# Batch 0's attention scores: key spans read in place from the whole keys, block maxima in a second product

## The chip, the cores and the metric

One core of one Trainium2 chip runs the kernel. A core has five engines with queues of their own: TensorE (PE in the profile, its weight loads PEld), VectorE (DVE), ScalarE (ACT), GpSimd (POOL) and SyncE (SP), which here only issues transfers. On-chip data lies in SBUF, 128 partitions wide; products land in PSUM, a small accumulator memory. The metric is the device time of one launch in microseconds (us), the median of several runs. The profile is that of one execution.

## The reference

Attention with a local window and a summary of every block, then a gated feed-forward layer with a short convolution:

```python
# q, k, v: (4 batches, 8 heads, 768 positions, 64), fp32
k_sum = k.reshape(B, H, 24, 32, D).max(axis=3)        # one key per block of 32
v_sum = v.reshape(B, H, 24, 32, D).mean(axis=3)
scores_l = scale * q @ k.T, kept where |pos_q - pos_k| < 16
scores_s = scale * q @ k_sum.T + log(32)
a = softmax(concat([scores_l, scores_s]))
x = (a @ concat([v, v_sum])) as (batch, position, 512)
h = relu(x @ w_in)                                    # 512 -> 1024
conv = 3-tap convolution of h along the positions, per channel
out = (h * sigmoid(conv)) @ w_out                     # 1024 -> 512
```

## The kernel before

**Chunks and pairs.** The work is cut into 8 chunks of 384 positions, two per batch (`c`, with `b, hf = divmod(c, 2)`). A chunk's attention goes over 4 pairs of heads (`p`), two heads on the two halves of the 128 partitions. A chunk of a pair has 6 query blocks of 64. A query block needs 96 keys around it (its span, `WK`) and the 24 block maxima (`NB`): 120 columns (`NK`).

**Scores.** Before the change every pair of every chunk has a tile `kw` of 6 x 120 columns: per query block its 96-key span, copied so that the spans overlap in memory, then the 24 maxima. In chunk 0 the spans are copied on chip from the whole keys of the pair (`k`, 784 columns, which lie in `spare`, borrowed space of the later tiles `xh` and `xl`) by DVE (pair 0) and POOL (pairs 1 to 3), at L213. From chunk 1 on SP loads them from memory with overlapping reads (L168). DVE reduces the whole keys to the maxima `ks` (L210) once per batch and pair; POOL copies these into all six blocks of `kw` (L217). `qk` then makes 12 products of 64 queries by 120 columns in fp32 (L260) into two PSUM tiles `pq`, one per head, of which two exist in all (tag `s`, `bufs=2`): the next pair's scores wait until DVE has read this pair's.

**After the scores.** DVE adds the mask and takes the maximum (L278), ACT does the exponentials (L288) and a small step for the sums (L296), DVE the reciprocal (L297), DVE (chunk 0) or POOL (later) the multiplication (L300). PE transposes the result (`pt`, L308), ACT or DVE copies it out (`aT`, L315, L313), and PE multiplies with the values (`xp`, L329). The output is split into two parts, `xh` and `xl`, for a three-product emulation of fp32 in the feed-forward layer: first layer `f1` (L404), the gate on ACT, DVE and POOL (L422 to L456), second layer `f2` (L473).

**Other work at the start.** The weights come as 64-bit words and are decoded and split on ACT, DVE and POOL (`decode`, L97 to L104, and `weights`, L127, L128): `w_in` in chunk 0's time, `w_out` in that of chunk 1. `warm` puts matmuls of zeros (`pw`, L78) between the others in chunk 0: 10 at the start, and some after each score, transpose and product.

**Order.** SP issues all loads of chunk 0 in the order of the string `LOADS` ("k0 q0 k1 q1 v0 k2 q2 a0 ..."). An attention step of half a pair has a slot `j`; a slot loads keys two pairs ahead, and makes the scores of its own pair. For chunks 0 and 1 a scheduler orders the instructions of every engine by its own estimates; from chunk 2 on PE's order is written out by hand (`manual_schedule`), the other engines' is still the scheduler's. A tile with `bufs=n` has n buffers that are handed round: the next user waits until the last reader is done.

```python
    spare = []
    for tag in ("xh", "xl"):
        t = sp.tile([P, 2, KL], F32, tag=tag, name=f"k_{tag}", bufs=2)
        spare += [t[:, 0, :], t[:, 1, :]]
```

Of the kernel before, what the change touches and what calls it, by code (L numbers as in the profile page):

```python
# [7 lines left out]
F32 = mybir.dt.float32  # L8
# [8 lines left out]
P = 128  # L17
WIN = 16
BLK = 32
NB = S // BLK  # L20
QB = 64
NQ = S // QB
WK = QB + 2 * WIN
NK = WK + NB
SP = S + 2 * WIN
NP = H // 2
CH = S // 2
CB = CH // QB
# [3 lines left out]
KL = S + WIN  # L32
# [18 lines left out]
def attention_ffn(ctx, tc, qT, kT, vT, v4, w_in, cwT, w_out, mask8, ident_in, out):  # L51
    nc = tc.nc
    cp = ctx.enter_context(tc.tile_pool(name="cp", bufs=1))
    sp = ctx.enter_context(tc.tile_pool(name="sp", bufs=2))
# [13 lines left out]

    idle = cp.tile([P, 512], mybir.dt.bfloat16, name="idle")
    nc.vector.memset(idle, 0.0)
    pw = ps.tile([P, 512], F32, tag="f2", name="pw", bufs=1)

    def warm(where, after=None):
        def go():
            for i in range(WARM.get(where, 0)):
                nc.tensor.matmul(pw, idle[:, :P], idle, start=True, stop=True)  # L78

        if after is None:  # L80
            go()
        else:
            with tc.issue_after(after):
                go()
# [48 lines left out]

    state = {}

    spare = []
    for tag in ("xh", "xl"):
        t = sp.tile([P, 2, KL], F32, tag=tag, name=f"k_{tag}", bufs=2)
        spare += [t[:, 0, :], t[:, 1, :]]

    def ins(x):
        return getattr(x, "ins", x)

    def window(ap, step, lead, run):

        return bass.AP(
            tensor=ap.tensor, offset=ap.offset, ap=[lead, [QB * step, CB], [1, run]]
        )

    def load_k(c, p):  # L150
        b, hf = divmod(c, 2)
        i = c * NP + p
        st = state[(c, p)] = {}
        if i == NP - 1:
            kw = sp.tile([P, 1024], F32, tag="stage", name=f"kw{i}", bufs=2)
            st["kw"] = kw[:, : CB * NK].rearrange("p (b k) -> p b k", b=CB)
        else:
            st["kw"] = sp.tile([P, CB, NK], F32, tag="kw", name=f"kw{i}", bufs=3)
        if hf == 0:
            if c == 0:  # L160
                k = spare[p]
            else:
                k = sp.tile([P, KL], F32, tag="kT", name=f"kT{i}", bufs=2)
            nc.sync.dma_start(k, kT[b, p, :, :KL])
            st["k"] = k
        if c:
            first = kT[b, p, :, hf * CH : hf * CH + WK]
            nc.sync.dma_start(st["kw"][:, :, :WK], window(first, 1, [SP, P], WK))  # L168

# [32 lines left out]
    def prep_pair(c, p):  # L202
        b, hf = divmod(c, 2)
        st = state[(c, p)]
        kw = st["kw"]
        if hf == 0:
            k = st["k"]
            ks = cp.tile([P, NB], F32, tag=f"ks{p}", name=f"ks{c * NP + p}")
            kv = k[:, WIN:KL].rearrange("p (n t) -> p n t", t=BLK)
            nc.vector.tensor_reduce(ks, kv, AX.X, ALU.max)  # L210
            state[("ks", b, p)] = ks
        if c == 0:
            (nc.gpsimd if p else nc.vector).tensor_copy(  # L213
                kw[:, :, :WK], window(k, 1, list(k.ap[0]), WK)
            )
        ks = state[("ks", b, p)]
        nc.gpsimd.tensor_copy(  # L217
            kw[:, :, WK:NK], ks.unsqueeze(1).to_broadcast([P, CB, NB])
        )

    def vmean_pair(c, p):

# [25 lines left out]
    def qk(c, p):  # L248


        st = state[(c, p)]
        n = c * NP + p
        pq = [
            ps.tile([P, 512], F32, tag="s", name=f"pq{n}_{h}", bufs=2) for h in range(2)
        ]
        for blk in range(CB):
            i, half = divmod(blk, 2)
            for h in range(2):
                r = slice(h * QB, (h + 1) * QB)
                last = nc.tensor.matmul(  # L260
                    pq[h][half * QB : (half + 1) * QB, i * NK : (i + 1) * NK],
                    st["q"][r, blk * QB : (blk + 1) * QB],
                    st["kw"][r, blk, :],
                    start=True,
                    stop=True,
                )
        if c == 0:
            warm(f"pq{p}", ins(last))
        softmax(n, c % 2, pq)

    def softmax(n, hf, pq):
        nm = sp.tile([P, 2, 3], F32, tag="nm", name=f"nm{n}", bufs=3)
        sm = sp.tile([P, 2, 3], F32, tag="sm", name=f"sm{n}", bufs=3)
        for h in range(2):
            a = sp.tile([P, 3, NK], F32, tag="a", name=f"a{n}_{h}", bufs=DEPTH + 2)
            state[("a", 2 * n + h)] = a
            for i in range(3):
                nc.vector.tensor_tensor_reduce(  # L278
                    a[:, i, :],
                    pq[h][:, i * NK : (i + 1) * NK],  # L280
                    mask[:, hf, i, :],
                    -0.125,
                    3.0e38,
                    ALU.add,
                    ALU.min,
                    nm[:, h, i : i + 1],
                )
                nc.scalar.activation(  # L288
                    a[:, i, :],
                    a[:, i, :],  # L290
                    AF.Exp,
                    bias=nm[:, h, i : i + 1],
                    scale=-1.0,
                    accum_out=sm[:, h, i : i + 1],
                )
        nc.scalar.activation(sm, sm, AF.Copy, bias=1e-9)  # L296
        nc.vector.reciprocal(sm, sm)  # L297
        for h in range(2):
            a = state[("a", 2 * n + h)]
            (nc.gpsimd if n >= NP else nc.vector).tensor_tensor(  # L300
                a, a, sm[:, h, :].unsqueeze(2).to_broadcast([P, 3, NK]), ALU.mult
            )
# [56 lines left out]
    def slot(j):  # L359

        if j % 2 == 0:
            n = j // 2 + 2
            if NP <= n < npair:
                load_k(*divmod(n, NP))
                load_vt(*divmod(n, NP))
            if NP <= j // 2 < npair:
                load_vm(*divmod(j // 2, NP))
            if j // 2 < npair:
                qk(*divmod(j // 2, NP))
        else:  # L370
            n = (j + 1) // 2
            if NP <= n + 1 < npair:
                load_q(*divmod(n + 1, NP))
            if n < npair:
                c, p = divmod(n, NP)
                if c:
                    vmean_pair(c, p)
                    load_v(c, p)
                prep_pair(c, p)
# [111 lines left out]
    for item in LOADS.split():  # L491
        what, n = item[0], int(item[1:] or 0)
        if what == "k":
            load_k(0, n)
        elif what == "q":
            load_q(0, n)
        elif what == "v":
            load_vt(0, n)
        elif what == "a":
            load_v(0, n)  # L500
        elif what == "w":
            raws[n] = load_in(n)
        else:
            nc.sync.dma_start(cw_words, cwT.bitcast(U32))

    prep_pair(0, 0)
    for j in range(2 * NP):
        slot(j)
# [177 lines left out]
```

## Time and profile before

| | |
|---|---|
| time, median of 3 runs | 404.95 us (404.81 to 405.63) |
| span of the profiled execution | 403.3 us |
| PE, busy share of the span | 96% |
| PE weight loads | 80% |
| DVE | 65% |
| ACT | 63% |
| POOL | 37% |
| transfers | 54.47 MB, mean 135 GB/s |

The span is the time from the first to the last instruction of one profiled execution; the time of a run is a little longer. A PE that is busy is not PE at its peak, since its matmuls overlap and their ends are modelled. In the rows of the profile an instruction stands as line, engine, operation, written tile <- read tiles, and what it waited for in brackets. A line number is that of the kernel before; L78 is the filler, L260 the scores, L404 and L473 the two layers.

### The profile page before, as it was taken

Reading aid. Unit: us, or ns where it says so; the run is one execution under the profiler, and the core shown is the slowest. Engines: PE = TensorE matmul, PEld = TensorE weight load, DVE = VectorE, ACT = ScalarE, POOL = GpSimd, SP = SyncE. Lnnn points to the kernel's source line nnn. Section 1 sums busy time; section 2 is a strip of 40 time slices with the busy share of each in tenths; the row PEclk is TensorE's granted clock in tenths of the full one; section 3 lists DMA queues with packets and bytes.
Section 4 is the critical chain, followed back from the end, with each engine's and each line's share of the span. In section 5 each row is a group of like instructions: output and inputs, shape, how many; then the busy total and the mean of one; then the engine's idle time right before and its main releaser. Section 6 shows DMA issues by size and latency. Waiting matters only on the chain.

```text
span 403.3 us, 8835 instructions
## 1 busy us (share of the span) xinstructions
PE 387.8 (96%) x3173; PEld 322.2 (80%) x3173; DVE 262.9 (65%) x777; ACT 255.8 (63%) x806; POOL 150.3 (37%) x179
## 2 busy tenths in 40 slices
PE   8989879999989999999999999999999999999996
PEld 3546558787768888888888888888888888999884
DVE  4889969998976665667765466466565655556200
ACT  3575699998876787766666778666666653343211
POOL 2316565377764234332333333332422242222200
PEclk9999799999899999999999999999999999999999
DMA  8999783666896784546233343334220000000011
GB/s 293 337 367 191 203 212 119 210 199 194 237 205 188 229 261 127 150 148 199 68 101 112 79 114 113 101 98 120 67 63 28 28 2 26 26 28 27 28 52 52
DMA packets 60715, 54.47 MB, mean 135 GB/s; under 512 B 24640, under 2 KB 51328, under 8 KB 60672
## 3 DMA queue, kind: packets, MB, share of 16 engines
q1 hardware_dynamic: 56928, 47.19, 41.2%
q10 hardware_dynamic: 3744, 6.73, 4.5%
q8 instruction: 25, 0.41, 0.5%
q14 instruction: 18, 0.15, 0.1%
HBM read 45.55 MB, written 6.29 MB: 129 GB/s over the span
## 4 chain that ended last, share of the span: by engine, by line
PE 85%; ACT 5%; DVE 3%; DMA 3%; POOL 2%; issue 1%; SPq 0%; DVEq 0%; POOLq 0%
PE f L473 33%; PE f L404 32%; PE pq L260 7%; PE xp L329 5%; PE pt L308 5%; PE pw L78 3%; ACT a L288 2%; DMA va<-v 2%; DMA k_xh<-kT 1%; POOL wout_lo L128 1%; DVE a L300 1%; POOL glo L456 0%; ACT wu_o L97 0%; ACT t L425 0%; PE pv L234 0%
## 5 line engine op out<-in xcount | busy, mean ns | idle before, releaser
L456 POOL TENSOR_TENSOR glo<-t,ghi 128x383 fp32r<-128x383 f32 (+1 forms) x64 | 66.3, 1037 | 138.3 <-ACT ghi L455 125.9
L404 PE MATMUL f<-xh,win_hi 128*128 128x384 f32 (+1 forms) x256 | 92.5, 361 | 0.9 <-ACT win_hi L127 0.9
L434 DVE SCALAR_TENSOR_TENSOR t<-f,cw,t 128x382 f32<-128x382 f32 (+3 forms) x128 | 78.8, 615 | 19.2 <-ACT t L425 16.6
L404 PE MATMUL f<-xl,win_hi 128*128 128x384 f32 (+1 forms) x256 | 87.9, 344 | 0.0
L404 PE MATMUL f<-xh,win_lo 128*128 128x384 f32 (+1 forms) x256 | 87.2, 341 | 0.0
L288 ACT ACTIVATE a<-a,nm 128x120 f32<-128x120 f32 x192 | 73.4, 384 | 12.3 <-DVE nm L278 12.1
L473 PE MATMUL f<-wout_lo,ghi 128*128 128x512 f32 x192 | 75.7, 394 | 1.6 <-POOL wout_lo L128 1.6
L473 PE MATMUL f<-wout_hi,ghi 128*128 128x512 f32 x192 | 76.4, 398 | 0.0
L473 PE MATMUL f<-wout_hi,glo 128*128 128x512 f32 x192 | 75.0, 391 | 0.0
L300 POOL TENSOR_TENSOR a<-a,sm 128x360 f32<-128x360 f32 x56 | 45.7, 837 | 45.6 <-ACT f L422 28.1
L451 ACT ACTIVATE t<-t 128x383 f32<-128x383 f32 (+1 forms) x64 | 33.6, 526 | 40.3 <-DVE t L434 39.6
L452 DVE SCALAR_TENSOR_TENSOR t<-t,f 128x383 f32<-128x383 f32 (+1 forms) x64 | 35.2, 552 | 29.6 <-ACT t L451 29.6
L404 PEld LDWEIGHTS f<-xh,win_hi 128*128 128x128 f32 x256 | 49.3, 192 | 5.1 <-ACT win_hi L127 1.2
L404 PEld LDWEIGHTS f<-xl,win_hi 128*128 128x128 f32 x256 | 49.2, 192 | 1.4 <-issue 0.3
L404 PEld LDWEIGHTS f<-xh,win_lo 128*128 128x128 f32 x256 | 48.9, 191 | 0.2
L278 DVE CUSTOM_DVE_ANT_0 a<-pq,mask 128x120 f32<-128x120 f32 x192 | 42.7, 275 | 1.5 <-PE pq L260 1.3
L473 PEld LDWEIGHTS f<-wout_lo,ghi 128*128 128x128 f32 x192 | 36.1, 188 | 7.9 <-POOL wout_lo L128 2.2
L473 PEld LDWEIGHTS f<-wout_hi,glo 128*128 128x128 f32 x192 | 36.1, 188 | 7.7
L473 PEld LDWEIGHTS f<-wout_hi,ghi 128*128 128x128 f32 x192 | 36.2, 188 | 7.0 <-issue 0.5
L315 ACT COPY aT<-pt 120x384 f32<-120x384 f32 x60 | 28.2, 470 | 20.7 <-PE pt L308 20.7
L422 ACT ACTIVATE f<-f 128x384 f32<-128x384 f32 (+1 forms) x64 | 30.4, 475 | 15.8 <-PE f L404 15.6
L308 PE MATMUL pt<-ident,a 128*120 128x128 f32 x192 | 33.7, 283 | 5.1 <-ACT aT L315 3.1
(59 smaller groups left out, 508.8 us busy)
## 6 DMA issues: line engine op xcount, KB each, us to landing
va<-v SPq DMA_DIRECT2D x32, 288.0 KB, 4.2
kw<-kT SPq DMA_DIRECT2D x28, 288.0 KB, 6.4
q<-qT SPq DMA_DIRECT2D x32, 192.0 KB, 4.5
out_dram<-ob ACTq DMA_DIRECT2D x24, 256.0 KB, 2.0
kT<-kT SPq DMA_DIRECT2D x12, 392.0 KB, 3.9
vt<-vT SPq DMA_DIRECT2D x12, 384.0 KB, 4.3
wo<-w_out SPq DMA_DIRECT2D x8, 512.0 KB, 5.3
raw_a<-w_in SPq DMA_DIRECT2D x6, 512.0 KB, 11.5
```

The source lines that it names most:

```text
L260: last = nc.tensor.matmul(pq[h][half * QB : (half + 1) * QB, i * NK : (i + 1) * NK], st["q"][r, blk * QB : (blk + 1) * QB], st["kw"][r, bl ...
L278: nc.vector.tensor_tensor_reduce(a[:, i, :], pq[h][:, i * NK : (i + 1) * NK], mask[:, hf, i, :], -0.125, 3.0e38, ALU.add, ALU.min, nm[:, h ...
L288: nc.scalar.activation(a[:, i, :], a[:, i, :], AF.Exp, bias=nm[:, h, i : i + 1], scale=-1.0, accum_out=sm[:, h, i : i + 1],)
L300: (nc.gpsimd if n >= NP else nc.vector).tensor_tensor(a, a, sm[:, h, :].unsqueeze(2).to_broadcast([P, 3, NK]), ALU.mult)
L308: last = nc.tensor.transpose(pt[:NK, i * P : (i + 1) * P], a[:, i, :], ident)
L404: last = nc.tensor.matmul(ph[:, :n], w[:, fc, cc, :], x[:, cc, :n], start=(cc == 0 and m == 0), stop=(cc == NCC - 1 and m == 2),)
L422: nc.scalar.activation(h[:, :n], h[:, :n], AF.Relu)
L434: nc.vector.scalar_tensor_tensor(t[:, i0:i1], h[:, hf + k - 1 + i0 : hf + k - 1 + i1], cw[:, fc, k : k + 1], t[:, i0:i1], ALU.mult, ALU.add,)
L451: nc.scalar.activation(t, t, AF.Tanh, scale=0.5)
L452: nc.vector.scalar_tensor_tensor(t, t, 1.0, h[:, hf : hf + ng], ALU.add, ALU.mult)
L456: nc.gpsimd.tensor_tensor(gated["lo"][:, fc, d0 : d0 + ng], t, hi.bitcast(F32), ALU.subtract)
L473: nc.tensor.matmul(po, gx[:, fc, ss], w[:, fc, :], start=(fc == 0 and m == 0), stop=(fc == NFC - 1 and m == 2),)
```

## The change

Batch 0 (chunks 0 and 1) has no `kw` any more. Its whole keys, all 800 columns with the margins, stay on chip for both chunks: pairs 0 and 1 in the two buffers of tag `kT`, pairs 2 and 3 in two of the three of tag `kw`. The scores are made in two products: 12 of 96 columns that read the span in place, then 12 of 24 columns that read `ks` itself, into the same places of `pq`. The span copies of chunk 0, the loads of chunk 1's spans and POOL's eight copies of the maxima for batch 0 go. From batch 1 on all is as before, except that `kT`'s and `kw`'s buffers first hold batch 0's keys. The tile of zeros for the filler shrinks from 512 to 128 columns, read four times over.

```diff
-    idle = cp.tile([P, 512], mybir.dt.bfloat16, name="idle")
+    idle = cp.tile([P, P], mybir.dt.bfloat16, name="idle")
...
-                nc.tensor.matmul(pw, idle[:, :P], idle, start=True, stop=True)
+                nc.tensor.matmul(
+                    pw.rearrange("p (r n) -> p r n", n=P),
+                    idle,
+                    idle.unsqueeze(1).to_broadcast([P, 4, P]),
...
-    spare = []
-    for tag in ("xh", "xl"):
-        t = sp.tile([P, 2, KL], F32, tag=tag, name=f"k_{tag}", bufs=2)
-        spare += [t[:, 0, :], t[:, 1, :]]
...  load_k
-        if i == NP - 1:
-            kw = sp.tile([P, 1024], F32, tag="stage", name=f"kw{i}", bufs=2)
+        if hf == 0:
+            tag, bufs = ("kw", 3) if b == 0 and p > 1 else ("kT", 2)
+            k = sp.tile([P, SP], F32, tag=tag, name=f"kT{i}", bufs=bufs)
+            n = SP if b == 0 else KL
+            nc.sync.dma_start(k[:, :n], kT[b, p, :, :n])
+            st["k"] = k
+        if b == 0:
+            st["k"] = state[(0, p)]["k"]
+        else:
+            kw = sp.tile([P, SP], F32, tag="kw", name=f"kw{i}", bufs=3)
             st["kw"] = kw[:, : CB * NK].rearrange("p (b k) -> p b k", b=CB)
-        else:
-            st["kw"] = sp.tile([P, CB, NK], F32, tag="kw", name=f"kw{i}", bufs=3)
-        if hf == 0:
-            if c == 0:
-                k = spare[p]
-            else:
-                k = sp.tile([P, KL], F32, tag="kT", name=f"kT{i}", bufs=2)
-            nc.sync.dma_start(k, kT[b, p, :, :KL])
-            st["k"] = k
-        if c:
             first = kT[b, p, :, hf * CH : hf * CH + WK]
             nc.sync.dma_start(st["kw"][:, :, :WK], window(first, 1, [SP, P], WK))
...  prep_pair
-        if c == 0:
-            (nc.gpsimd if p else nc.vector).tensor_copy(
-                kw[:, :, :WK], window(k, 1, list(k.ap[0]), WK)
-            )
-        ks = state[("ks", b, p)]
-        nc.gpsimd.tensor_copy(
-            kw[:, :, WK:NK], ks.unsqueeze(1).to_broadcast([P, CB, NB])
-        )
+        ks = state[("ks", b, p)]
+        if b:
+            nc.gpsimd.tensor_copy(
+                st["kw"][:, :, WK:NK], ks.unsqueeze(1).to_broadcast([P, CB, NB])
+            )
...  qk
+        if b == 0:
+            def near(r, blk):
+                at = hf * CH + blk * QB
+                return st["k"][r, at : at + WK]
+            ks = state[("ks", b, p)]
+            parts = [(0, WK, near), (WK, NK, lambda r, blk: ks[r, :])]
+        else:
+            parts = [(0, NK, lambda r, blk: st["kw"][r, blk, :])]
+        for first, end, keys in parts:
+            for blk in range(CB):
...
```

The scheduler makes another order of chunks 0 and 1 from this. Three places of it follow, with the tile's number behind each name (so `pq_0_132` is a score tile of the first head, `a_0` the softmax of the first head of a pair, `f_0_2` the first layer of chunk 0, block 2). The first is PE in chunk 0, the scores of the third pair (`q_2`) and the transposes of the first pair's two heads. Before:

```order
L78 MATMUL pw<-idle 128x512
L260 MATMUL pq_0_257<-kw_100,q_2_102 64x120
L308 MATMUL pt_235<-ident,a_0_153 120x128 x3
L78 LDWEIGHTS idle
...
L260 MATMUL pq_1_258<-kw_100,q_2_102 64x120
L260 MATMUL pq_0_257<-kw_100,q_2_102 64x120
...
L234 MATMUL pv_1_230<-ident,vs_1_228 24x128
L260 MATMUL pq_1_258<-kw_100,q_2_102 64x120
L308 MATMUL pt_247<-ident,a_1_160 120x128 x3
```

And the same place now:

```order
L78 MATMUL pw<-idle 128x512
L317 MATMUL pt_253<-ident,a_0_161 120x128 x3
L78 LDWEIGHTS idle
...
L267 MATMUL pq_0_271<-kT_98,q_2_100 64x96
L267 MATMUL pq_1_272<-kT_98,q_2_100 64x96
...
L229 MATMUL pv_1_248<-ident,vs_1_246 24x128
L267 MATMUL pq_1_272<-kT_98,q_2_100 64x96
L317 MATMUL pt_263<-ident,a_1_168 120x128 x3
```

The one product of the third pair that stood alone ahead of the first transposes has moved behind them, to the others; the 24-column products (`pq<-ks`) of this pair come after the second transposes.

The second place is SP's queue after the loads of `LOADS`: the span loads of chunk 1 before,

```order
L110 DMA raw_b<-w_in 128x1024 x2
L168 DMA kw_255<-kT 128x6x96
L185 DMA q_0_329<-qT 128x384
L168 DMA kw_343<-kT 128x6x96
L185 DMA q_1_415<-qT 128x384
L193 DMA va_417<-v 96x6x128
L168 DMA kw_521<-kT 128x6x96
L198 DMA va_417<-vm_0_175 24x6x128
```

and what follows there now:

```order
L116 DMA raw_b<-w_in 128x1024 x2
L184 DMA q_0_355<-qT 128x384
L184 DMA q_1_449<-qT 128x384
L192 DMA va_451<-v 96x6x128
L197 DMA va_451<-vm_0_183 24x6x128
L184 DMA q_2_601<-qT 128x384
```

The `kw` loads are gone, and queries and values have moved up by their places.

The third place is PE in chunk 1, around the scores of its third pair (`q_2`), with the first layer of chunk 0, blocks 1 and 2. Before:

```order
L404 MATMUL f_0_1_505<-xh_325,win_lo 128x384
L78 LDWEIGHTS idle
...
L404 MATMUL f_0_2_764<-xl_326,win_hi 128x384
L404 MATMUL f_0_2_764<-xh_325,win_lo 128x384
L308 MATMUL pt_600<-ident,a_0_540 120x128 x3
L404 MATMUL f_0_2_764<-xh_325,win_hi 128x384
...
L308 MATMUL pt_643<-ident,a_1_547 120x128 x3
L260 MATMUL pq_0_667<-kw_521,q_2_558 64x120
```

And now:

```order
L413 MATMUL f_0_1_538<-xh_351,win_lo 128x384
L78 LDWEIGHTS idle
...
L267 MATMUL pq_0_718<-kT_98,q_2_601 64x96
L317 MATMUL pt_652<-ident,a_0_583 120x128 x3
L267 MATMUL pq_0_718<-kT_98,q_2_601 64x96 x2
...
L267 MATMUL pq_0_718<-ks_261,q_2_601 64x24
...
L413 MATMUL f_0_2_826<-xh_351,win_hi 128x384
```

The third pair's scores have moved from behind most of block 2 of the first layer, and behind the transposes of both heads, to just behind block 1.

More of the change, by code (lines that the diff above doesn't have):

```diff
@@ L77, in go @@
             for i in range(WARM.get(where, 0)):
-                nc.tensor.matmul(pw, idle[:, :P], idle, start=True, stop=True)
+                nc.tensor.matmul(
+                    pw.rearrange("p (r n) -> p r n", n=P),
+                    idle,
+                    idle.unsqueeze(1).to_broadcast([P, 4, P]),
+                    start=True,
+                    stop=True,
+                )
         if after is None:
@@ L204, in prep_pair @@
         st = state[(c, p)]
-        kw = st["kw"]
         if hf == 0:
@@ L255, in qk @@
         ]
[L256 to L265, printed above, removed]
-                )
+        b, hf = divmod(c, 2)
+        if b == 0:
[8 more added lines that the diff above has]
+            for blk in range(CB):
+                i, half = divmod(blk, 2)
+                for h in range(2):
+                    r = slice(h * QB, (h + 1) * QB)
+                    last = nc.tensor.matmul(
+                        pq[h][
+                            half * QB : (half + 1) * QB, i * NK + first : i * NK + end
+                        ],
+                        st["q"][r, blk * QB : (blk + 1) * QB],
+                        keys(r, blk),
+                        start=True,
+                        stop=True,
+                    )
         if c == 0:
```

## The prediction

> **What bounds the kernel now.** I read the page first, then the stages, then the chain of waits over the first 30 us, then TensorE's (PE) timeline. The page:
>
> ```profile
> span 403.3 us, 8835 instructions
> PE 387.8 (96%) x3173; PEld 322.2 (80%) x3173; DVE 262.9 (65%) x777; ACT 255.8 (63%) x806; POOL 150.3 (37%) x179
> ```
>
> The sum below is made against this execution, 403.3 us of span; the median of the runs shown is 404.95 us, so 1.65 us lies around the span and is added at the end. The stages (us from:to, then length, busy time of PE, PE weight loads, DVE, ACT, POOL, the granted clock, DMA share, GB/s):
>
> ```profile
> 0.00:24.00 24.00, 22.17 (x179) 10.70 (x179) 16.55 (x58) 11.87 (x49) 6.66 (x15) 1.00 0.98 318
> 24.00:46.00 22.00, 17.31 (x176) 11.63 (x176) 20.98 (x61) 13.81 (x46) 10.47 (x9) 0.97 0.92 251
> 46.00:60.00 14.00, 11.06 (x109) 8.39 (x107) 10.54 (x38) 10.88 (x40) 7.96 (x9) 0.80 0.81 217
> 60.00:95.00 35.00, 35.00 (x340) 27.80 (x338) 33.12 (x96) 31.90 (x106) 21.35 (x25) 1.00 0.55 170
> 95.00:125.00 30.00, 27.62 (x212) 21.97 (x211) 23.87 (x69) 24.98 (x76) 18.96 (x17) 0.94 0.87 225
> 125.00:403.00 278.00, 274.58 (x2167) 241.70 (x2165) 157.88 (x458) 162.37 (x494) 84.88 (x105) 1.00 0.31 92
> ```
>
> From 125 us on PE is the bound (a busy 274.6 of 278), with a fixed order that the change does not touch. So only one thing matters: when PE gets there. Ahead of it PE has no idle from 60 to 95, DVE is the bound from 24 to 46 (20.98 of 22), and from 46 to 60 nobody is: PE idles 2.94, DVE 3.46, ACT 3.12 us, at a clock of 0.80. Everything that the change removes lies in chunks 0 and 1, ahead of 60 us. The chain there:
>
> ```profile
> 0.74 3.98 DMA k_xh<-kT
> ...
> 4.74 0.96 DVE ks L210
> ...
> 5.76 0.47 POOL kw L217
> ...
> 6.28 1.48 PE pq L260 x24
> 7.75 2.25 PE pw L78 x5
> 10.00 1.30 PE pq L260 x23
> ...
> 11.73 2.37 PE pw L78 x11
> 14.10 0.35 PE pq L260 x2
> 14.45 0.47 PE pt L308 x3
> ...
> 15.93 0.35 PE pq L260 x2
> 16.28 0.49 PE pt L308 x3
> ...
> 16.79 0.56 DVE aT L313
> 17.34 1.03 DVE a L300 x2
> ```
>
> The first keys land at 4.72; reduction and copy hold PE until 6.28; then the chain runs through PE, filler matmuls (pw) included, until 16.79, and DVE takes it. Five fillers take 2.25 us before 10 us and eleven take 2.37 after it: 0.45 against 0.215 us each, so PE ran at half clock until about 10.5 us (the stage row's 1.00 does not show it).
>
> **The change part by part.**
>
> *Front.* The near product needs only k and q; the sums wait for the reduction alone. How early can it start?
>
> ```profile
> 1.19 4.45 PE L78 MATMUL pw<-idle 128*128 128x512 bf16 x10 [1.19 <-DVE idle L72]
> ...
> q<-qT SPq DMA_DIRECT2D x32, 192.0 KB, 4.5
> ```
>
> The ten fillers end at 5.64, less about 0.15 for a shorter zero fill (a quarter of the elements). q is issued behind k, at about 1.2 us; at the median 4.5 us it lands at 5.7. Start 5.65 instead of 6.28: **-0.65 us**. The bounds are 5.5 and 6.28 (q late).
>
> *Split product.* Per pair, 24 matmuls of 120 columns become 24 of 96 and 24 of 24 (each fp32 product is two records).
>
> ```profile
> 15.28 0.43 PE L260 MATMUL pq<-kw,q 64*64 64x120 f32 x8
> ...
> 19.18 0.92 PE L329 MATMUL xp<-aT,va 120*64 120x64 f32 x24
> ...
> 28.53 0.30 PE L329 MATMUL xp<-aT,va 120*64 120x64 f32 x2 [0.28 <-POOL va L238]
> ...
> 39.58 0.85 PE L260 MATMUL pq<-kw,q 64*64 64x120 f32 x24
> ```
>
> At full clock one more 120-column matmul costs (0.85 - 0.43)/16 = 26 ns, so a pair's 24 take 0.63; at 96 columns, in proportion, 0.50. No row has 24 columns. From below, in proportion to columns: 0.13, no extra cost. From above, the price of xp's matmuls, (0.92 - 0.30)/22 = 28 ns each: 0.67, an extra of 0.54 per pair. xp has two tiles of the array at work, these have four, and the same 64 weight columns to load, so I take half, 0.34: **+0.2 us a pair**, twice that at half clock. Pairs 0 and 1 stand on the chain at half clock (pair 1 in part): **+0.5 us** (0 to +1.6). In chunk 0's third pair the order changes too: the two matmuls that stood alone ahead of the first transposes (0.35 us, against 0.05 within a run) join the others: **-0.3 us**. Pair 3 comes after 16.79, where DVE has the chain. Pairs 4 to 7 stand ahead of PE waits:
>
> ```profile
> 43.54 0.83 PE L260 MATMUL pq<-kw,q 64*64 64x120 f32 x12 [1.95 <-issue]
> ...
> 59.74 0.52 PE L308 MATMUL pt<-ident,a 128*120 128x128 f32 x3 [2.79 <-ACT aT L315]
> ```
>
> Two waits of 1.95 and 2.79 us hide their 0.8 us; should both waits go, it is on the path.
>
> *Copies that go.* The span copies (three on POOL, one on DVE) and eight copies of the block maxima on POOL:
>
> ```profile
> 5.61 0.45 DVE L213 COPY kw<-k_xh 128x576 f32<-128x576 f32 x1
> 6.67 0.95 DVE L210 TENSOR_REDUCE ks<-k_xh 128x24 f32<-128x768 f32 x1 [0.61 <-DMA k_xh<-kT]
> ...
> 12.63 1.64 DVE L300 TENSOR_TENSOR a<-a,sm 128x360 f32<-128x360 f32 x2
> ```
>
> ```profile
> 13.14 0.75 POOL L213 COPY kw<-k_xl 128x576 f32<-128x576 f32 x1 [0.16 <-DMA k_xl<-kT]
> ...
> 41.68 0.76 POOL L217 COPY kw<-ks 128x144 f32<-128x144 f32 x1
> ```
>
> ```profile
> 42.65 0.27 DVE L278 CUSTOM_DVE_ANT_0 a<-pq,mask 128x120 f32<-128x120 f32 x1
> ```
>
> The DVE copy stands where DVE next waits for k1 (its reduction at 6.67): 0. At 12.63 two multiplies took 1.64 us beside POOL's copy, and 1.03 at 17.34 without one; that 0.6 is not on the chain, since PE reaches those transposes later: 0. The copy at 41.68 is named as PE's releaser at 43.54, but it ended at 42.44. What ended in time was DVE's read of the pair before (DVE's score read began at 42.65), because the score tiles have two buffers. That wait stays: 0.
>
> *Transfers.* Four span loads (288 KB) leave SP's queue in chunk 1; q, va and the next k move up. The new k of batch 1, pair 0, now needs the buffer of chunk 0's first k, free when chunk 1's first scores are done (39.58 + 0.85); SP issued it at 42.91 before, so no loss. But DVE's reduction of it now stands ahead of the reads of chunk 1's third scores. It landed at about 46.8 (42.91 and a median of 3.9, below); DVE, from its read at 42.65, has twelve reads and four weight steps ahead of it, an estimated 4 to 5 us: 0, with +1 us if the load is late.
>
> ```profile
> kT<-kT SPq DMA_DIRECT2D x12, 392.0 KB, 3.9
> ...
> 42.91 0.51 SPq L164 DMA_DIRECT2D kT<-kT  x1
> ```
>
> *Carry.* By 16.79 the sum is -0.65 + 0.5 - 0.3 = **-0.45 us**, and DVE, without gaps to 46 us, carries it.
>
> *46 to 60 us.* Two things here. PE's clock:
>
> ```profile
> 45.00:50.00 5.00, 5.00 (x24) 3.64 (x21) 4.25 (x17) 2.77 (x16) 2.26 (x2) 0.50 0.74 217
> 50.00:55.00 5.00, 4.86 (x64) 4.03 (x63) 2.52 (x12) 4.11 (x12) 3.91 (x4) 0.85 0.83 221
> ...
> 52.17 0.85 PE L260 MATMUL pq<-kw,q 64*64 64x120 f32 x24
> ```
>
> It fell to half right after the 1.95 us wait, which costs (0.50 + 0.15) x 5 = 3.25 us of PE work while DVE and ACT ran short. And the order: chunk 1's third scores (52.17) now stand ahead of the third block of the first layer, right behind the second pair's, so that their softmax fills the holes of DVE and ACT. The gain ends where the first of them is full, ACT's 3.12 us; nothing (0) if the clock still falls and the new order only shifts the wait. I take 0.7 of it, nearer the full end, since both causes of the holes are reduced: **-2.2 us**. PE has no idle from 60 to 95, so this carries. In 95 to 125 the instructions are the same in slightly other order: 0, with +-1 us, since its waits are for split weights, which ACT and DVE make.
>
> Sum: 403.3 - 0.45 - 2.2 = 400.65 of span; with 1.65 around it, **402.3 us**.
>
> [...] PE's longest wait ahead of the clock's fall was 1.95 us, and the fall came with it. [...]
>
> **Rivals.**
> 1. *The small product costs as much as a middling one* (ends slower). If each 24-column matmul takes 28 ns like xp's, a pair costs +0.54, at half clock double. Pairs 0 and 1: +1.6 on the chain instead of +0.5; then PE is +0.65 late at 16.79 (-0.65 + 1.6 - 0.3), and in chunk 1 four pairs add 2.2 us, of which the waits hide about half if the clock falls again. No gain in 46 to 60. Time 404.95 + 0.65 + 1.1 = 406.7. It decides from about 20 ns per small matmul, where the front's gain is gone. For it: xp, 64 columns, costs more per matmul than 120 columns here. Against: four tiles work at once. [...]
> 2. *Hidden anyway.* The 0.45 us is lost in a wait before 60 us and the clock falls as before: 404.5 to 405, no change. For it: from 24 to 46 DVE is full with splits of weights that did not change. Against: the holes in 46 to 60 are not DVE's work.
> 3. *The clock holds all the way.* The front gap shrinks from 0.64 to about 0.1 us, so the half clock may end earlier: the five fillers then save up to 5 x 0.235 = 1.2 us; the wait at 43.54 shrinks below what halves the clock, and ACT's 3.12 us are gained whole. 404.95 - 0.45 - 1.2 - 3.1 = 400.2. Against: q may land late.
> That the change does not do what it says is no rival: the new order has no span copy for batch 0.
>
> **How the numbers follow.** 0.2% of 404.95 is 0.8 us, about what a measurement of this kernel can tell from no change. The forecast (400.8 to 404.1 us) has 0.52, rival 3 (below 400.8) 0.12, rival 2 (404.1 to 405.8) 0.19, rival 1 (above 405.8) 0.17. Faster 0.64, same 0.19, slower 0.17. For 8 in 10 the range leaves out a tail below 400.2 and half of rival 1: 400.2 to 406.2; the forecast's own range is 400.8 to 404.1.
>
> **What would show it.** PE's first score matmul at 5.6 to 5.7 us, the split pair at about 1.05 us at full clock, the second transposes' copy on DVE at 16.3 or earlier; chunk 1's third scores near 48 us instead of 52.17, ACT full from 46 to 58, and a clock in 45:50 above 0.5. Wrong would be: small matmuls at 25 ns or more each, the clock halved for longer than 6.5 us in chunk 1, or PE idle above 2.4 us in 95 to 125.

## The result, and the profile after

The changed kernel takes 407.4 us (median; 406.31 to 409.63), the kernel before, on the same chip, 405.37 us. The ratio is 1.0073, with a 95% interval of 1.0044 to 1.0102: slower, where 402.3 us was forecast, and above the whole range. The ratio is formed from the fast runs and need not be the quotient of the two medians, which is 1.0050. The page of its profiled execution (407.15 us, span 405.0 us):

```profile
span 405.0 us, 9196 instructions
PE 386.4 (95%) x3365; PEld 322.5 (80%) x3365; DVE 260.3 (64%) x776; ACT 256.4 (63%) x806; POOL 142.5 (35%) x168
```

The copies are gone from POOL (150.3 to 142.5 us busy), and PE has 192 more matmuls, which is 96 products of two records. The stages, in the columns of the prediction's table:

```profile
24.00:46.00 22.00, 17.09 (x248) 11.80 (x238) 18.71 (x55) 13.04 (x39) 8.03 (x7) 1.00 1.03 293
46.00:60.00 14.00, 12.47 (x178) 8.72 (x173) 12.77 (x41) 12.05 (x45) 8.99 (x10) 0.88 0.75 190
60.00:95.00 35.00, 34.71 (x330) 27.83 (x331) 30.93 (x96) 31.77 (x105) 18.90 (x24) 0.95 0.65 187
95.00:125.00 30.00, 25.66 (x193) 19.38 (x192) 26.45 (x73) 24.34 (x73) 18.97 (x19) 1.00 0.66 192
```

Three things stand against the rows of before. DVE, which was busy 20.98 of the 22 us from 24 to 46, is busy 18.71. In 46 to 60 PE is fuller (12.47 against 11.06) at a higher clock (0.88 against 0.80), as forecast. But 60 to 95, which had PE full at a clock of 1.00, now has 0.95, and in 95 to 125 PE has 4.3 us of idle against 2.4. PE's timeline shows the places; a number in brackets is the idle time in front of the row:

```profile
5.53 0.73 PE L267 MATMUL pq<-kT,q 64*64 64x96 f32 x24
6.04 0.52 PE L267 MATMUL pq<-ks,q 64*64 64x24 f32 x24
6.50 0.82 PE L78 MATMUL pw<-idle 128*128 128x512 bf16 x3
...
44.84 0.71 PE L267 MATMUL pq<-kT,q 64*64 64x96 f32 x12 [3.29 <-issue]
...
50.25 0.62 PE L267 MATMUL pq<-kT,q 64*64 64x96 f32 x17
...
59.63 0.33 PE L338 MATMUL xp<-aT,va 120*64 120x64 f32 x2 [1.50 <-DVE xl L359]
...
61.49 0.69 PE L413 MATMUL f<-xh,win_hi 128*128 128x384 f32 x1
...
113.11 0.50 PE L482 MATMUL f<-wout_lo,ghi 128*128 128x512 f32 x1 [2.33 <-POOL wout_lo L134]
```

The front starts at 5.53 us instead of 6.28. The wait ahead of chunk 1's second scores has grown from 1.95 to 3.29 us, and the long waits at 59.63 and 113.11 were 2.79 and 1.03 us in about the same places. The clock in two windows of the same profile:

```profile
45.00:50.00 5.00, 5.00 (x59) 3.24 (x58) 4.86 (x22) 5.00 (x25) 3.07 (x4) 0.66 0.84 197
60.00:65.00 5.00, 4.71 (x21) 3.93 (x22) 5.00 (x20) 3.27 (x11) 2.12 (x2) 0.66 0.26 91
```

The clock still halves behind the first wait, for 3.4 us here (6.8 us before), and now also behind the second (60.0 to 63.5 us). Before, the wait at 59.74 had no such consequence. DVE's timeline shows why the front's lead did not reach chunk 1:

```profile
7.55 0.95 DVE L208 TENSOR_REDUCE ks<-kT 128x24 f32<-128x768 f32 x1 [1.91 <-DMA kT<-kT]
...
14.10 0.95 DVE L223 TENSOR_REDUCE vs<-raw_b 128x24 f32<-128x768 f32 x1 [0.41 <-DMA raw_b<-vT]
15.65 0.95 DVE L208 TENSOR_REDUCE ks<-kT 128x24 f32<-128x768 f32 x1 [0.60 <-DMA kT<-kT]
...
16.61 0.51 DVE L322 COPY aT<-pt 120x384 f32<-120x384 f32 x1
...
21.20 0.95 DVE L223 TENSOR_REDUCE vs<-raw_b 128x24 f32<-128x768 f32 x1 [1.97 <-DMA raw_b<-vT]
27.11 0.95 DVE L223 TENSOR_REDUCE vs<-raw_b 128x24 f32<-128x768 f32 x1 [1.12 <-DMA raw_b<-vT]
...
44.06 0.27 DVE L287 CUSTOM_DVE_ANT_0 a<-pq,mask 128x120 f32<-128x120 f32 x1
```

DVE waits for transfers that came in time before, or nearly so:

```profile
14.20 0.94 DVE L228 TENSOR_REDUCE vs<-raw_b 128x24 f32<-128x768 f32 x1
...
19.52 0.94 DVE L228 TENSOR_REDUCE vs<-raw_b 128x24 f32<-128x768 f32 x1
```

From 4 to 46 us DVE is idle for 8.9 us, against 4.7 before. (The 12.0 and 7.1 us in the expectations below also hold the wait for the first keys, most of which lies ahead of 4 us.) At 16.61 us the changed kernel is 0.18 us ahead (16.79 before), at chunk 1's first scores 1.41 us behind (44.06 against 42.65).

### The profile page after: what moved, and what is told of

Read it like the earlier page. It is cut to its first block, busy times and chain, and to the rows that moved or that the text cites. A ratio compares the mean times of both kernels' runs of the same rounds, so it can differ in the third digit from the quotient of the medians.

```text
span 405.0 us, 9196 instructions
## 1 busy us (share of the span) xinstructions
PE 386.4 (95%) x3365; PEld 322.5 (80%) x3365; DVE 260.3 (64%) x776; ACT 256.4 (63%) x806; POOL 142.5 (35%) x168
## 4 chain that ended last, share of the span: by engine, by line
PE 81%; DMA 9%; ACT 4%; DVE 3%; issue 1%; POOL 1%; SPq 0%; ACTq 0%
PE f L482 32%; PE f L413 31%; PE xp L338 6%; DMA va<-v 5%; PE pq L267 5%; PE pt L317 5%; DMA raw_b<-w_in 2%; PE pw L78 2%; ACT a L297 1%; DMA mask<-mask 1%; DVE wu_o L107 1%; POOL wout_lo L134 1%; POOL a L309 1%; ACT aT L324 0%; DVE t L443 0%
## 5 line engine op out<-in xcount | busy, mean ns | idle before, releaser
L465 POOL TENSOR_TENSOR glo<-t,ghi 128x383 fp32r<-128x383 f32 (+1 forms) x64 | 65.4, 1022 | 142.4 <-ACT ghi L464 131.0
L464 ACT CAST ghi<-t 128x383 fp32r<-128x383 f32 (+1 forms) x64 | 32.5, 508 | 8.7 <-DVE t L461 8.5
```

The lines of the kernel that those rows point to most:

```text
L464: nc.scalar.copy(hi, t)
L465: nc.gpsimd.tensor_tensor(gated["lo"][:, fc, d0 : d0 + ng], t, hi.bitcast(F32), ALU.subtract)
```

## The experiments

Two theories at first. A: the transfers of the start are slower (A1: because of the change, A2: from execution to execution) and DVE pays. B: the split product and the order that the scheduler makes from it lose the time.

**The two kernels once more, unchanged.**

> The kernel before, unchanged, profiled once more. Question: do the slow transfers of the start belong to the changed kernel, or to the execution that was profiled? In the first profile of the kernel before, 5:25 us moved 348 GB/s and the fourth pair's keys were reduced at 13.0 us. Theory A1 (the changed transfers make the start slow): again 340 to 355 GB/s. Theory A2 (speed differs from execution to execution): anything from 285 to 350, and DVE's gaps from 4 to 46 us move with it (7.1 us in the first profile).

> The changed kernel, unchanged, profiled once more. Its first profile had 290 GB/s in 5:25 us, 12.0 us of DVE gaps from 4 to 46 us and PE at half clock in 60.0 to 63.5 us. Theory A1: again 280 to 300 GB/s and 11 to 13 us of gaps. Theory A2: the rate may be near 340, then the gaps are 7 to 9 us and the span 403 to 404. Theory B (the new order and the dearer product lose the time, whatever the transfers do): half clock again near 60 us, span 404.5 to 406 at any rate.

The kernel before moved 335 GB/s in 5:25 us, with 3.8 us of DVE's idle time from 4 to 46 us; the changed kernel 290 GB/s again, with 7.9 us, the wait of 3.29 us and the halved clock at 60 us. Times 403.74 and 409.04 us. The 335 GB/s lie just below what A1 expected and within A2's range, and the changed kernel's span of 406.9 us lies just above B's. Two profiles point to A1 and B, but rule out nothing.

**Keys of 784 columns instead of whole rows.**

```diff
-            nc.sync.dma_start(k[:, :n], kT[b, p, :, :n])
+            nc.sync.dma_start(k[:, :KL], kT[b, p, :, :KL])
+            if b == 0:
+                nc.gpsimd.memset(k[:, KL:SP], 0.0)
```

> The changed kernel with batch 0's keys loaded as 784 columns as before (rows of 3136 bytes instead of 3200, which are the whole row in memory); GpSimd zeroes the last 16 columns, which the mask hides. Theory A1 with the row's shape as cause: 5:25 us back at 340 GB/s or more, DVE's gaps down to about 7 to 8 us, 2 to 4 us less time than the changed kernel, ratio to the kernel before 0.995 to 1.000. If the row's shape is nothing: 280 to 300 GB/s and ratio 1.005 to 1.010, as the changed kernel. Theory B: ratio 1.005 to 1.010 in both cases.

Ratio 0.9998 (0.9969 to 1.0027), 404.66 us: the time of the kernel before. But the transfers stayed at 292 GB/s and DVE's idle time from 4 to 46 us at 7.5 us. The time fell by 2.7 us and the reason given for it was wrong; theory B, which had 1.005 to 1.010 here too, missed as well. What else differs: the scheduler prices a smaller load lower, and its order is another; on DVE it departs from the changed kernel's at 60 us. The waits ahead of that are still there (3.28 us at 42.70, 1.49 at 58.76), with the halved clock behind each, but from 95 to 125 us PE idles 2.2 instead of 4.3 us:

```profile
95.00:125.00 30.00, 27.85 (x208) 21.85 (x208) 27.25 (x76) 25.99 (x76) 20.88 (x20) 1.00 0.69 210
```

**The split product alone.** In the kernel before, for chunks 0 and 1:

```diff
-        for blk in range(CB):
+        for first, end in ((0, WK), (WK, NK)) if c < 2 else ((0, NK),):
+            for blk in range(CB):
...
-                    st["kw"][r, blk, :],
+                        st["kw"][r, blk, first:end],
```

> The kernel before with one part of the change: batch 0's scores in two products (96 and 24 columns), both read from the copied spans as before; copies, transfers and filler stay. Theory A: the second product costs the predicted 0.2 us a pair and little of it shows: ratio 0.999 to 1.003, 5:25 us at 340 to 355 GB/s. Theory B: the product and the order made from it are what loses the time: ratio 1.005 to 1.012 here too.

Ratio 1.0032 (0.9996 to 1.0069), between the two expectations: inconclusive on the time. Its transfers ran at 294 GB/s, although they are those of before:

```profile
5.00:25.00 20.00, 17.77 (x268) 11.27 (x270) 16.12 (x71) 11.67 (x53) 6.73 (x11) 1.00 1.08 294
```

(The third-last column is the clock, the second-last the DMA share, the last GB/s.) This looked like a slowdown of the transfers by PE's many small matmuls; the next runs tested that, and the order.

**Keys of 798 columns.** As with 784, with `n = 798` and the last two columns zeroed.

> The changed kernel with batch 0's keys loaded as 798 columns and the last two zeroed on GpSimd: 3192 bytes, no longer the whole row in memory, yet the scheduler's order of VectorE is the changed kernel's word for word and that of TensorE but for 10 lines. (With 784 columns the order came out another.) Theory row: the whole 3200-byte row costs what 784 columns saved; ratio 0.997 to 1.003, like 784 columns. Theory order: the 2.8 us between 800 and 784 columns are the other order that follows from the load's estimated price; then ratio 1.005 to 1.010, as the changed kernel, the same waits of TensorE (3.3 us near 44 us, 1.5 near 60, 2.3 near 113).

Ratio 1.0060 (1.0028 to 1.0093), and the waits of the changed kernel near 44 and 60 us (3.29 and 1.49); the third, near 113 us, was 0.82 instead of the expected 2.3. Theory row falls. With 784 columns the ratio is lower by 0.6%, and the order is the difference between the two that is left to explain it.

**More, smaller fillers in the kernel before.**

```diff
-                nc.tensor.matmul(pw, idle[:, :P], idle, start=True, stop=True)
+                for s in range(4):
+                    nc.tensor.matmul(pw[:, s * P : (s + 1) * P], idle[:, :P],
+                                     idle[:, s * P : (s + 1) * P], start=True, stop=True)
```

> The kernel before with each filler matmul of 512 columns cut into four of 128: the same columns, about 150 more matmuls in chunk 0, no split scores. Question: why do the transfers run at 290 instead of 335 to 348 GB/s in 5:25 us in all kernels with split scores? Theory instructions (many more TensorE instructions in that time slow the transfers): 280 to 305 GB/s here too. Theory split (something else in the split product): 330 to 350 GB/s.

316 GB/s, between both expectations, at 407.64 us (one run). Alone it settles nothing; the control below settles more.

**22 fillers where PE waits in chunk 1, in both kernels.**

```diff
-        if c == 0:
-            warm(f"pq{p}", ins(last))
+        if c < 2:
+            warm(f"pq{c * NP + p}", ins(last))
...  WARM
-"pq3": 3, "tr": 2
+"pq3": 3, "pq4": 14, "pq7": 8, "tr": 2
```

> The changed kernel with 14 more filler matmuls behind the scores of chunk 1's first pair and 8 behind those of its last, where TensorE waits 3.3 and 1.5 us and its clock then falls to half. Theory clock (the changed kernel loses its time through halved windows of 3.4 us, about two more than the kernel before): mean granted clock from 0.981 to 0.990 or more, ratio 0.993 to 1.000. Theory DVE (late transfers set the end of chunk 1, the clock only follows): the clock rises, the time does not, ratio 1.003 to 1.010.

> The kernel before with the same 22 fillers, as control for the run above. Theory clock: clock from 0.989 to 0.993 or more and ratio 0.992 to 0.999; against the changed kernel with the same fillers it is 0 to 2 us slower. Theory DVE: ratio 0.998 to 1.003.

The changed kernel fell by 3.3 us, to 404.14 us, ratio 1.0007 (0.9973 to 1.0042); its mean granted clock rose from 0.981 to 0.988. The kernel before rose to 406.56 us, ratio 1.0070 (1.0035 to 1.0104), although its clock rose too, from 0.989 to 0.992. None of the four ranges of the ratio was met, neither theory clock's nor theory DVE's. So the clock is not all: the fillers make another order, with a new wait, in both kernels. The control's, and then the changed kernel's:

```profile
49.84 0.90 PE L308 MATMUL pt<-ident,a 128*120 128x128 f32 x3 [3.61 <-POOL a L300]
```

```profile
51.16 0.89 PE L317 MATMUL pt<-ident,a 128*120 128x128 f32 x3 [3.41 <-POOL a L309]
```

Since both have it, this wait does not tell why one kernel gained and the other lost.

The control also has the program of before, unchanged, to about 40 us. Its 5:25 us, and those of the first profiles of before and of the changed kernel, in this order:

```profile
5.00:25.00 20.00, 17.44 (x182) 9.46 (x182) 16.20 (x69) 11.60 (x53) 6.57 (x11) 1.00 1.07 298
```

```profile
5.00:25.00 20.00, 19.05 (x176) 9.83 (x174) 17.02 (x66) 11.10 (x51) 6.46 (x11) 1.00 1.07 348
```

```profile
5.00:25.00 20.00, 17.10 (x266) 10.40 (x265) 14.76 (x60) 10.03 (x47) 2.82 (x3) 1.00 1.08 290
```

The same instructions and transfers ran at 298 GB/s here and at 348 there: the rate differs from execution to execution, and A1 in its strict form falls. A tendency is left: over all runs here, five profiles with the start of before have 298 to 348 (mean 320), nine with the changed start 281 to 308 (mean 294), and three more of the changed kernel with one filler fewer in that time 284, 312 and 314. The ranges overlap.

**Other orders of both kernels.** What the 784 columns and the control had in common was another order. A third width, `n = 792`, and one filler fewer behind the third pair's scores, in the changed kernel:

```diff
-"pq2": 3
+"pq2": 2
```

> The changed kernel with batch 0's keys loaded as 792 columns, the last eight zeroed on GpSimd. It is nothing but a third order: the scheduler's order is the changed kernel's to about 55 us, then differs from it (106 lines on VectorE) and from that of 784 columns (101). Theory scatter (the change itself is worth about nothing to -1 us; which order of 55 to 125 us the scheduler happens to make decides by +-2 us): anything from 0.997 to 1.010, and the time is explained by TensorE's waits after 55 us. Theory cost (the change itself costs 2 us): 1.004 to 1.010.

> The changed kernel with one filler matmul fewer behind the third pair's scores of chunk 0 (two instead of three, 0.2 us), which makes another order from 24 us on (216 lines on VectorE). In the kernel before the same edit leaves VectorE's order as it was. Theory scatter: 0.996 to 1.010; theory cost: 1.004 to 1.010.

Ratios 1.0032 (1.0000 to 1.0063) and 1.0046 (1.0010 to 1.0082). And in the kernel before, one filler fewer per block (`"unit": 2`), or behind the second pair's scores (`"pq1": 11`):

> The kernel before with two instead of three fillers per block of the first layer in chunk 0: another order from about 50 us on (106 lines on VectorE). Theory scatter: orders of the kernel before scatter as those of the changed one do; 0.997 to 1.008, most likely above 1.002, since the order of before is a good draw. Theory cost: 0.997 to 1.002.

> The kernel before with one filler fewer behind the second pair's scores (11 instead of 12): another order from about 22 us on (159 lines on VectorE). Theory scatter: 0.997 to 1.008, most likely above 1.002. Theory cost: 0.997 to 1.002.

Ratios 1.0060 (1.0026 to 1.0094) and 1.0113 (1.0050 to 1.0176). The second has six runs, the others twelve. The kernel before, with one tiny edit that has nothing to do with the change, is about as slow as the changed kernel. Theory cost had 0.997 to 1.002 for both, and falls.

**Five pairs.** The two filler edits in the changed kernel, and one more edit in both:

```diff
-OUT_AT = (6, 7, 8, 9, 10, 10, 11, 12)
+OUT_AT = (5, 6, 7, 8, 9, 10, 11, 12)
```

> The changed kernel with two instead of three fillers per block of the first layer in chunk 0, the pair of the same edit in the kernel before, which came out at 1.0060. Theory order: 0.997 to 1.010, on either side of 1.0060 with equal chance. Theory cost (the change costs about 2.4 us whatever the order): 1.009 to 1.014.

> The changed kernel with 11 instead of 12 fillers behind the second pair's scores, the pair of the same edit in the kernel before, which came out at 1.0113. Its order is nearly that of the changed kernel with one filler fewer behind the third pair's scores (1.0046). Theory order: 1.001 to 1.009, below its pair. Theory cost: 1.013 to 1.019.

> The changed kernel with the weights of the second layer fetched and split one unit earlier for all but the last two blocks that shared a unit. Theory order: 0.997 to 1.010, sign against its pair open. Theory cost: 0.004 to 0.008 above its pair.

> The kernel before with the same edit. Theory order: 0.998 to 1.010, most likely above 1.002, since the order of before has been the best of its kind so far. Theory cost: 0.997 to 1.004.

All ratios are to the kernel before without edit, with 95% intervals:

| edit | kernel before | changed kernel | difference |
|---|---|---|---|
| none | 1 | 1.0073 (1.0044 to 1.0102) | +0.73% |
| 22 fillers in chunk 1 | 1.0070 (1.0035 to 1.0104) | 1.0007 (0.9973 to 1.0042) | -0.63% |
| two fillers per block | 1.0060 (1.0026 to 1.0094) | 1.0064 (1.0037 to 1.0091) | +0.04% |
| 11 fillers behind pair 1 | 1.0113 (1.0050 to 1.0176) | 1.0037 (1.0008 to 1.0065) | -0.76% |
| weights one unit earlier | 1.0016 (0.9982 to 1.0049) | 0.9994 (0.9964 to 1.0025) | -0.22% |
| mean | 1.0052 | 1.0035 | -0.17% |

Theory cost missed in each of the three new pairs. The differences scatter by 0.6% about a mean of -0.17%, whose standard error from the five is 0.27%. The sign goes both ways: which order an edit draws moves the time by more than the change does. Whether the change by itself is worth anything, five pairs can't tell; their 95% interval goes from -0.9 to +0.6%. Nor are all the edits neutral: the 22 fillers were put where the changed kernel waits. The kernel before without edit is nominally the best of its five orders and the changed kernel without edit the worst of its five, though the next in line lies within the noise of each.

The last edit also shows one place that the order costs. Its first 60 us are those of the changed kernel, waits included:

```profile
43.16 0.75 PE L267 MATMUL pq<-kT,q 64*64 64x96 f32 x12 [3.30 <-issue]
...
59.45 0.33 PE L338 MATMUL xp<-aT,va 120*64 120x64 f32 x2 [1.50 <-DVE xl L359]
```

```profile
95.00:125.00 30.00, 28.82 (x219) 23.18 (x219) 27.34 (x71) 24.58 (x71) 20.34 (x21) 1.00 0.73 216
```

PE idles 1.2 us in 95 to 125 instead of 4.3, and the median is 404.63 instead of 407.4 us. The wait for split weights at 113.11 is not the change's own; it goes when DVE and ACT begin the weights one unit earlier.

**Both mended at once.** The weights one unit earlier, with 11 fillers behind pair 1, and with 784 columns:

> The changed kernel with the second layer's weights one unit earlier (alone 0.9994, TensorE idle 1.2 us in 95 to 125) and 11 instead of 12 fillers behind the second pair's scores (alone 1.0037; its wait near 44 us was 1.7 instead of 3.3 us). If the two places are independent: TensorE idle below 1.5 us in 95 to 125, the first wait 1.7 us, ratio 0.992 to 0.998. If every edit is a new draw of the order: 0.997 to 1.008.

> The changed kernel with the second layer's weights one unit earlier and 784 key columns (alone 0.9998). Independent: ratio 0.993 to 0.999. A new draw: 0.997 to 1.008.

Ratios 0.9965 (0.9932 to 0.9998) and 0.9987 (0.9958 to 1.0015), on a chip with the kernel before at 403.83 us; times 402.80 and 403.26 us. The first lies below the kernel before, by little; the independent places were expected at 0.992 to 0.998, a new draw at 0.997 to 1.008. The second fits both expectations. The stages of the first:

```profile
46.00:60.00 14.00, 11.46 (x200) 8.82 (x200) 12.77 (x55) 12.98 (x53) 9.40 (x11) 1.00 0.89 234
95.00:125.00 30.00, 28.06 (x204) 22.02 (x205) 27.94 (x76) 24.93 (x73) 19.31 (x19) 1.00 0.69 200
```

The first wait was 1.74 us, as expected, and the clock did not halve in 46 to 60, but it did later (0.95 in 60 to 95). In 95 to 125 there are 1.9 us of idle where below 1.5 was expected for independent places. It is also the best of some ten orders of the changed kernel, and its interval barely leaves out 1, so a gain is not shown.

## Why the prediction was wrong, step by step

**Front: right at the start, lost by 17 us.** PE began at 5.53 us (5.65 forecast). But the second transposes' copy came at 16.61, not at 16.3 or earlier, and even the 0.18 us of lead were not the change's. The clock was full at 5.44 us instead of 10.58; that looks like rival 3's early clock, but three of the five profiles with the start of before had it too (full from 5.0, 5.2 and 6.2 us). In these DVE's copy of the second transposes came at 15.34 to 15.93 us, those of the changed start with a clock full by 6.2 us and up to the copy at 15.89 to 17.20 (seven profiles, mean 16.3). The earliest, from the second profile of the kernel before:

```profile
15.34 0.56 DVE L313 COPY aT<-pt 120x384 f32<-120x384 f32 x1 [0.76 <-PE pt L308]
```

There DVE waited for PE. In the changed kernel's profile the copy has no wait in front, since DVE itself was late with the fourth pair's keys (15.65, behind a wait for their transfer). So the first step of the prediction that failed is its *Carry*: "By 16.79 the sum is -0.65 + 0.5 - 0.3 = **-0.45 us**, and DVE, without gaps to 46 us, carries it". It put the transfers of the start at nothing. DVE had no gaps because transfers that filled 0.98 of the DMA engines came just in time; at 290 GB/s they did not, and DVE waited for keys and for `vT`. Over the profiles with the same start DVE reads chunk 1's first scores at 41.2 to 43.4 us (mean of five 42.5, kernel before) and at 41.9 to 44.6 us (mean of nine 43.3, changed): about 0.8 us late instead of 0.45 early, with wide scatter. Why the changed start tends to the lower rates is open; split scores without the rest of the change have 294 GB/s, cut fillers 316, and neither tells.

**The wait ahead of chunk 1's second scores: forecast to stay, longer by 1.3 us.** The prediction has "That wait stays: 0". Late transfers do not set its length: in all eight profiles with the changed kernel's order of DVE up to there it is 3.28 to 3.30 us, at 281 to 308 GB/s, and in the kernel before and two of its orders (four profiles) 1.92 to 2.22 us, at 304 to 348. The split product alone has 3.43 us; with one filler fewer in chunk 0 the changed kernel has 1.72 and 1.73, and 1.74 at 284 GB/s where the weights come one unit earlier as well. So its length goes with the order of the instructions. Which place of the order makes it is not worked out.

**Split product: right.** From the first near product to the next instruction a pair takes 6.50 - 5.53 = 0.97 us, before 40.35 - 39.58 = 0.77: +0.2 a pair. What the terms for the first three pairs (+0.5 and -0.3) came to can't be told apart from the late transfers. The end of that interval, and a later row, from PE's timeline of the kernel before:

```profile
40.35 0.44 PE L404 MATMUL f<-xh,win_hi 128*128 128x384 f32 x1
...
60.80 0.44 PE L404 MATMUL f<-xh,win_hi 128*128 128x384 f32 x1
```

The sizes inside were off. 24 matmuls of 96 columns take 6.04 - 5.53 = 0.51 us, as estimated, and 24 of 24 columns 6.50 - 6.04 = 0.46, not 0.34: 19 ns each, against 21 for four times the columns, and close to rival 1's 20 ns from which the front's gain would be gone.

**Copies, and the new keys of chunk 1's time: 0, right.** No wait of DVE in 46 to 62 us is for a transfer. At the start it was otherwise, as said: the second keys were reduced at 7.55 us instead of the 6.67 that the prediction kept.

**46 to 60 us: fuller, but hardly earlier.** PE's idle in this stage fell from 2.94 to 1.53 us, and the clock took (1 - 0.88) x 14 = 1.7 us instead of 2.8: together 2.5 us, near the forecast's 2.2. That is not what PE got ahead by. The second scores began 1.30 us later than before (44.84, 43.54), the first layer's fourth block 0.69 us later (61.49, 60.80), so the stretch between made good 0.6 us of the forecast's 2.2. Chunk 1's third scores came 1.9 us earlier, but because the new order has them earlier.

The next sentence that failed is "PE has no idle from 60 to 95, so this carries". The clock halved again behind the 1.50 us wait at 59.63, which takes (1 - 0.95) x 35 = 1.75 us in 60 to 95. That wait was shorter than the 2.79 us of before, which halved nothing. The fifth block begins 1.83 us later than before:

```profile
64.53 0.42 PE L404 MATMUL f<-xh,win_hi 128*128 128x384 f32 x1
```

```profile
66.36 0.42 PE L413 MATMUL f<-xh,win_hi 128*128 128x384 f32 x1
```

**95 to 125 us: 0 here, but +-1 was too narrow.** PE's idle is 4.3 us; before it was 2.4 with 1.7 lost to halved clock, which is about as much, and the changed kernel is 1.74 us late at 104 us and again at 130. Other executions and orders differ more: the changed kernel's second profile has 4.0 us of idle and 1.7 lost to halved clock, the one with the weights one unit earlier 1.2 and none.

**The sum over the two profiles.** The same matmul of PE comes 1.30 us later than before at chunk 1's second scores, 0.69 at 61 us, 1.74 at 104 us and 1.79 at the end: +1.3, -0.6, +1.05 and 0, where the prediction had -0.45, -2.2, 0 and 0. This is one pair of executions; the second profile of the kernel before is 1.5 us shorter than its first, that of the changed kernel 1.9 us longer.

**The clock, where the sum of it is seen.** The runs of the kernel before that stood beside these experiments go with their granted clock: a median of 402.0 us at 0.994 and more, 403.9 at about 0.992 and 406.0 at about 0.987. Their slope is 0.80 us of time for each us of clock lost. The changed kernel's clock is 0.981 on the mean of its runs, 7.7 us lost, against 4.3 for those runs: at that slope 2.7 us, nearly its whole loss (0.73% are 3.0 us). But this is a correlation, and it does not hold within the changed kernel: its own nine runs have a slope of 0.36, which makes 1.2 us, and its run at 0.991 took 407.15 us, 3 us more than the kernel before at such a clock. Which wait halves the clock looks partly like chance, as two orders show that are all but the same here (one filler fewer behind pair 2, and behind pair 1):

```profile
44.02 0.71 PE L267 MATMUL pq<-kT,q 64*64 64x96 f32 x12 [1.72 <-issue]
...
45.00:50.00 5.00, 4.14 (x91) 3.13 (x86) 4.52 (x19) 5.00 (x24) 3.23 (x3) 1.00 0.86 185
```

```profile
43.31 0.71 PE L267 MATMUL pq<-kT,q 64*64 64x96 f32 x12 [1.73 <-issue]
...
45.00:50.00 5.00, 5.00 (x63) 3.39 (x60) 3.89 (x17) 4.47 (x20) 3.21 (x3) 0.69 0.67 156
```

The same wait, 1.72 and 1.73 us, and the clock holds in the first (1.00 in 45 to 50) and halves in the second (0.69). With 11 fillers and the weights one unit earlier a wait of 1.74 us halved nothing either (1.00 in 46 to 60). In each of the first profiles of the two kernels the changes of the clock stand 3.41 us or multiples of it apart: at 44.72, 51.54, 102.74 and 106.16 us before, at 46.40, 49.81, 60.05 and 63.46 us in the changed kernel. Counted on in such steps, the 2.79 us of before fall into two stretches, with 1.42 and 1.37 us, and the clock held; the 1.50 us of the changed kernel lie in one, from 56.64 to 60.05 us, and it halved. But that is not all of it. The four stretches that half clock followed had 1.95 and 0.80 us of PE's idle time before (from 41.30 and 99.33 us), 1.86 and 1.58 us in the changed kernel (from 42.98 and 56.64 us). In the changed kernel the stretch from 111.25 us had 1.87 us, and the clock held. What decides is open.

**Rivals.** Rival 1's time (406.7) was nearest, by the wrong mechanism: no pair cost more than forecast. Rival 3's early clock came, but the kernel before has it in some executions too. None had what the runs showed: another order with other waits, drawn by an edit that changes the scheduler's prices. Of the prediction's signs of being wrong two came, half clock for 6.8 us in all behind the two waits of chunk 1 and PE idle of 4.3 us in 95 to 125. The 0.2% that it took as telling from no change was too small: the intervals here are +-0.3% and more.

What stays open: why the transfers tend to be slower with the changed start, and what the change would be worth with the order held still. Of the latter the five pairs give -0.17%, with a standard error of 0.27%.

## What to carry to other kernels

Where a scheduler makes the order from estimated prices, an edit is also a new draw of the order, and here draws differ by up to 1%, more than the pairs show the edit to be worth. Before a small difference is put down to the change, give both kernels the same three or four harmless edits and compare the pairs. A gain is followed to the next wait of the bound engine and through it: a stage that was fuller by 2.5 us made good only 0.6 us, and a halved clock behind the next wait cost more than that; an engine "without gaps" was so by the grace of transfers that filled 0.98 of the DMA engines and came just in time.

## What the runs showed of the hardware

- The same transfers, issued by the same instructions, ran at 298 to 348 GB/s in 5:25 us from one execution to the next (five profiles), with a DMA share of 1.07 or 1.08 in all of them.
- Behind a wait of 1.50 us PE's clock was at half for 3.41 us (60.05 to 63.46 us, changed kernel); behind one of 2.79 us, at 59.74 us in the kernel before, it held. In each of these two profiles the changes of the clock lie 3.41 us or a multiple of it apart. Half clock followed stretches of that length with 0.80 to 1.95 us of PE's idle time (four), and one with 1.87 us was followed by full clock.
- Matmuls of 24 columns on four 64x64 tiles cost 19 ns each, those of 96 columns 21 ns (24 of each, from 5.53 to 6.50 us in the changed kernel's profile; from 39.34 to 40.31 us there it is 18 and 22.5 ns).
